# A gated linear recurrence before a mixture of experts: the next chunk's state summed by accumulating transfers, earlier due times, earlier fills

## The chip, the core and the metric

The kernel runs on one core of one Trainium2 chip. A core has TensorE (matrix products, PE in the profile), VectorE (DVE), ScalarE (ACT), GpSimd (POOL) and SyncE (SP); each executes its own instructions in order and waits on semaphores for the others. Transfers between memory and the on-chip buffers run beside them on 16 transfer engines. SyncE and GpSimd issue them here, each into a queue of its own. The metric is the time of the whole program on the device in microseconds; lower is better.

## The reference

```python
# B, H, S, D = 4, 8, 768, 48
mag = np.sqrt(a_re * a_re + a_im * a_im)
scale = np.minimum(mag, 0.999) / (mag + 1e-06)
a_re_n, a_im_n = (a_re * scale, a_im * scale)
for t in range(S):
    new_re = ar * S_re - ai * S_im          # ar, ai: a_re_n, a_im_n at t, per key dimension
    new_im = ar * S_im + ai * S_re
    S_re, S_im = (new_re + kv, new_im)      # kv: outer product of k[t] and v[t]
    y[:, :, t] = np.einsum('bhd,bhde->bhe', q[:, :, t], S_re)
...
# x: y with the heads side by side, [3072, 384]; E = 8 experts, F = 1024, cap = 768
logits = x @ w_gate
expert_idx = np.argmax(logits, axis=1)      # one expert for a token, gate_w its probability
h = np.maximum(np.einsum('ecd,edf->ecf', disp, w1), 0.0)
y = np.einsum('ecf,efd->ecd', h, w2)
out[i] = gate_w[i] * y[expert_idx[i], pos[i]]
```

The recurrence has a complex factor for each key dimension and step. Everything is float32.

## The kernel before

**Chunks and groups.** The 768 steps are cut into 8 chunks of 96 (C), two to a group, so there are four groups (0 to 3). Inside a chunk the cumulative products of the complex factors are taken outward from the chunk's middle, so that q and k can be multiplied by them and the chunk's output becomes a masked matrix product, as in linear attention. Real and imaginary parts lie side by side: 48 real and 48 imaginary rows of a state make 96 partitions.

**Slices.** For a group, all batches, heads and both directions fill 128 partitions, and the 48 steps outward are done in six slices of 8 (`SIZES`). A slice goes through `norm` (line 278: load of the factors `a`, the clipped scale by squares, logarithm and exponential on ScalarE, sums by TensorE against the identity, products on VectorE), `scan` (line 371: eight dependent complex products, lines 394 and 399, on VectorE) and `post` (line 413: q and k times the products or their inverses, lines 442 and 477 on VectorE, then writes to a scratch tensor in memory, lines 485 to 499, issued by GpSimd). The last slice's products are also taken aside by `pend` (line 524), which makes of them the factors `pcol` that carry a state into the next chunk (lines 567 to 572).

**Units.** A unit (line 576) is one chunk of one batch: 8 units to a group, 32 in all. SyncE loads its q and k from the scratch tensor (line 593), v and the middle row; TensorE turns q and k (619), multiplies them (635), VectorE masks the product (639), and TensorE multiplies that with v (700) and q with the incoming state z (705). Chunk c's state is `s` (650 on TensorE, plus z on VectorE in 659). For the next chunk it is multiplied by a complex factor: two transfers issued by SyncE exchange the real and the imaginary half into `sx` (663), `u` is s times the real factor (671 on ScalarE, eight instructions; 668 on VectorE where the next chunk is in the last group), `sx` is multiplied by the imaginary factor (674, VectorE), and the sum of both is the next z (677, VectorE). This happens 28 times: chunks 0 to 6 of four batches. A chunk's z is read four units later. In an odd chunk it needs the `pcol` of the next group, so at the border between two groups the states are carried over only when the next group's scan is done.

**Experts.** Each finished unit is routed; GpSimd sends its token rows to the buffer `disp` in memory by an indirect transfer (1007). That buffer is first filled with empty rows in seven transfers of 772 KB (`fill`, line 846), issued by GpSimd. Then the eight experts run (from line 1176 on), their weights split into two parts by ScalarE and VectorE (1112, 1113), and are bound to TensorE's work (1203, 1211, 1224).

**What sets the order.** A planner (class `Plan`) lists every operation of the attention part with an engine, an assumed duration, its predecessors, the buffers that it shares and a due time, `want`; it simulates the engines and writes the resulting order into the program. Among operations that could start at about the same time the one due earlier goes first. An operation that issues a transfer (one with `kb`) is also not placed before its due time; the others may go earlier. Due times hang on `BEGIN`: the scan of group g is due from BEGIN[g] to BEGIN[g+1], the units of group g from BEGIN[g+1] + 8 on, and the last entry sets the experts' first weight loads (BEGIN[4] + 26) and the routing's last steps. `fill_gaps` puts in matrix products of no use (line 226) where the plan shows TensorE idle, to keep it running. On the chip the engines execute this order whatever the plan's times were.

Of the kernel before, what the change touches and what calls it, by code (L numbers as in the profile page):

```python
# [18 lines left out]
C = 96  # L19
# [161 lines left out]
class Att:  # L181
# [96 lines left out]
    def norm(self, g, j, s0):  # L278
# [6 lines left out]
        w = s0 - 14  # L285
# [11 lines left out]
        def xa():  # L297
            a4 = self.tile_a4(g, j)
            sq = st['sq'] = a4[:, 0:n, 0:2, :].rearrange("p i z d -> p z i d")
            nc.scalar.activation(sq, st['a'], AF.Square, accum_out=self.sums[g][:, 0, j:j + 1])  # L300
        o = plan.op(K + ("xa",), "ACT", act(2 * n * D) + .1, xa, w, after=[K + ("load",)], bufs=[a_, a4_])
        if g == 0 and j < 1:
# [4 lines left out]
            o = plan.op(None, "DVE", dve(n * D), xb, w, after=[o], bufs=[a4_])  # L307
            parts = [(0, n, o, a4_)]
# [215 lines left out]
    def pend(self, g, want):  # L524
# [36 lines left out]
        def cols():  # L561
            pr = self.p_t.tile([C, 2, B, H], F32, tag="vgp", name=f"vgp_{g}", bufs=1)
            for i in range(int(g == 0), G2):
# [8 lines left out]
                nc.vector.tensor_tensor(out=p[1], in0=p[1], in1=pr[:, 1], op=ALU.subtract)  # L572
# [3 lines left out]
    def unit(self, g, i, w, per, near):  # L576
# [84 lines left out]
        def swap(i):  # L661
            a, o = ((slice(0, D), slice(D, None)), (slice(D, None), slice(0, D)))[i]
            nc.sync.dma_start(out=st['sx'][a], in_=st['s'][o])

        def turn():
            u = st['u'] = self.p_c.tile([C, H, D], F32, tag="u", name=f"u_{b}_{c}", bufs=2)
            if nx // G2 == NG - 1:
                nc.vector.tensor_tensor(out=u, in0=st['s'], in1=pc(0).unsqueeze(2).broadcast_to([C, H, D]), op=ALU.mult)
                return
            for h in range(H):  # L670
                nc.scalar.mul(out=u[:, h, :], in_=st['s'][:, h, :], mul=pc(0)[:, h:h + 1])  # L671

        def state_a():
            nc.vector.tensor_tensor(out=st['sx'], in0=st['sx'], in1=pc(1).unsqueeze(2).broadcast_to([C, H, D]), op=ALU.mult)

        def state_b():
            nc.vector.tensor_tensor(out=zn[:C], in0=st['u'], in1=st['sx'], op=ALU.add)
# [3 lines left out]
        if not last:  # L681
# [3 lines left out]
            x = [plan.op(None, "SP", .55, lambda i=i: swap(i), w - 20, after=[d], bufs=[R("s_sb"), R("sx")], kb=72, extra=5.) for i in range(2)]  # L685
# [3 lines left out]
            u = plan.op(None, "DVE" if late else "ACT", dve(384) if late else 1.8, turn, wz, after=[d, pcn], bufs=[R("s_sb"), R("u")])  # L689
            za = plan.op(None, "DVE", dve(384), state_a, wz, after=x + [pcn], bufs=[R("sx")])  # L690
            plan.op(K("ZB"), "DVE", dve(384), state_b, wz + 2, after=[u, za], bufs=[R("sx"), R("u"), ("z", b, c + 1)])
# [59 lines left out]
RINGS = dict(qkc=3, v=3, qT=2, kT=2, a_sb=2, z=5, s_sb=4, sx=4, u=2, xt=2, tr=2, pa=2, s=1, ad=2, y=1,  # L751
# [847 lines left out]
```

## Time and profile before

| | us |
|---|---|
| time, median of 3 runs (635.39 to 637.35) | 635.4 |
| the profiled execution, its own time | 635.5 |
| its span, from first to last instruction | 633.7 |

| engine | busy us | share of the span | instructions |
|---|---|---|---|
| TensorE | 560.3 | 88% | 4740 |
| VectorE | 473.1 | 75% | 1356 |
| ScalarE | 384.8 | 61% | 1034 |
| GpSimd | 161.7 | 26% | 237 |

The shares are averages over stages with different limits, so the stage in which something lies has to be looked at by itself. In the chain of waits a piece is a time on an engine or in a transfer that the next piece waited for. A transfer's time to landing runs from its issue to its last byte. The mean granted clock of TensorE is 0.962 of full speed.

### The profile page before, as it was taken

The page shows a single profiled execution, that of the slowest core. Times are in us where ns is not written, and L with a number is a line of the kernel's source. Part 1 is how long each engine was busy: PE and PEld are TensorE (multiplying, and loading weights), DVE is VectorE, ACT ScalarE, POOL GpSimd, SP SyncE. Part 2 cuts the span into 40 slices and gives each one's busy share as a digit, 9 for nine tenths or more (in the row PEclk, how much of TensorE's full clock was granted, in tenths as well). Part 3 has the DMA queues.
Part 4 walks back from the last instruction along what each step waited for, and adds up shares of the span by engine and source line. Part 5 has one row for each costly group of instructions (what it writes and reads, how often), then busy time and mean ns, then how long its engine had stood idle before and what let it go on. Part 6 is the DMA issues. An engine that isn't in the chain of part 4 may idle for free.

```text
span 633.7 us, 13410 instructions
## 1 busy us (share of the span) xinstructions
PE 560.3 (88%) x4740; PEld 489.7 (77%) x4740; DVE 473.1 (75%) x1356; ACT 384.8 (61%) x1034; POOL 161.7 (26%) x237
## 2 busy tenths in 40 slices
PE   2355389899999999999989999999999999999992
PEld 1122267687787877878879987999999999999992
DVE  3999978899999999999976564455755565556541
ACT  6566658888989789987555642353434444444530
POOL 2554331231235732244210521002020111202012
PEclk9776689999999999999999999999999999999997
DMA  4378699978767977778669931634545554544301
GB/s 140 88 205 262 178 266 287 218 203 221 182 185 225 265 207 198 186 200 197 150 157 223 289 103 29 207 106 134 150 141 173 160 160 150 154 152 138 100 37 38
DMA packets 75627, 108.80 MB, mean 172 GB/s; under 512 B 11715, under 2 KB 65852, under 8 KB 75552
## 3 DMA queue, kind: packets, MB, share of 16 engines
q1 hardware_dynamic: 61776, 61.50, 35.7%
q0 software_dynamic: 13776, 46.37, 25.7%
q8 instruction: 39, 0.64, 0.4%
q14 instruction: 36, 0.29, 0.2%
HBM read 71.51 MB, written 32.47 MB: 164 GB/s over the span
## 4 chain that ended last, share of the span: by engine, by line
PE 48%; DVE 27%; DMA 10%; ACT 9%; issue 3%; SPq 1%; POOL 1%; POOLq 0%; DVEq 0%; ACTq 0%
PE ph L1203 17%; PE my L1211 15%; DVE xy L394 5%; DVE a L399 3%; DMA qkc<-scr 3%; DVE qko L442 2%; DVE qko L477 2%; PE my L1224 2%; ACT u L671 2%; DMA sx<-s 2%; PE pa L635 2%; DMA scr<-qko 2%; DVE a_sb L639 2%; PE tr L619 2%; PE yt L1157 1%
## 5 line engine op out<-in xcount | busy, mean ns | idle before, releaser
L1249 ACT ACTIVATE hh<-ph 128x448 fp32r<-128x448 f32 (+7 forms) x64 | 32.6, 510 | 92.2 <-PE ph L1203 92.2
L1250 DVE SCALAR_TENSOR_TENSOR hl<-ph,hh 128x448 fp32r<-128x448 f32 (+7 forms) x64 | 37.2, 581 | 60.3 <-ACT hh L1249 59.6
L1113 DVE TENSOR_TENSOR lo<-raw,hi 128x384 fp32r<-128x384 f32 (+2 forms) x128 | 65.5, 553 | 7.0 <-ACT hi L1112 7.0
L1203 PE MATMUL ph<-xh,hi 128*128 128x448 f32 (+7 forms) x192 | 69.7, 363 | 0.0
L1168 POOL DMA_INDIRECT out_dram<-o,xr x26 | 25.7, 987 | 162.0 <-DVE o L1167 158.6
L1203 PE MATMUL ph<-xh,lo 128*128 128x448 f32 (+7 forms) x192 | 66.6, 347 | 0.0
L272 PE MATMUL n<-a,ident 128*128 128x384 f32 x92 | 41.8, 587 | 25.3 <-ACT a L300 19.2
L394 DVE TENSOR_TENSOR xy<-a 128x192 f32<-128x192 f32 (+1 forms) x193 | 60.4, 324 | 1.7 <-ACT a L364 1.1
L1112 ACT CAST hi<-raw 128x384 fp32r<-128x384 f32 (+2 forms) x128 | 59.0, 512 | 4.0 <-DMA raw<-in_moe_w_dram 4.0
L1211 PE MATMUL my<-hh,lo 128*128 128x448 f32 (+6 forms) x168 | 58.7, 350 | 0.0
L1211 PE MATMUL my<-hh,hi 128*128 128x448 f32 (+6 forms) x168 | 58.7, 349 | 0.0
L1211 PE MATMUL my<-hl,hi 128*128 128x448 f32 (+6 forms) x168 | 58.7, 349 | 0.0
L635 PE MATMUL pa<-qT,kT 128*96 128x96 f32 x512 | 54.5, 251 | 1.1 <-DVE a_sb L639 1.0
L619 PE MATMUL tr<-ident,qkc 81*96 81x81 f32 x512 | 52.1, 237 | 3.8 <-ACT ends L517 1.0
L1007 POOL DMA_INDIRECT disp<-x,idx x32 | 39.3, 1228 | 63.0 <-DVE idx L1003 28.3
L635 PEld LDWEIGHTS pa<-qT,kT 128*96 128x96 f32 x512 | 48.8, 165 | 3.1 <-DVE a_sb L639 1.3
L619 PEld LDWEIGHTS tr<-ident,qkc 81*96 81x96 f32 x512 | 41.2, 127 | 12.1 <-ACT kT L623 2.4
L399 DVE TENSOR_TENSOR a<-xy 128x96 f32<-128x96 f32 (+1 forms) x213 | 48.7, 238 | 0.7
L272 PEld LDWEIGHTS n<-a,ident 128*128 128x128 f32 x92 | 19.1, 226 | 38.4 <-ACT a L300 21.0
L272 PE MATMUL p<-qko,ident 128*128 128x384 f32 x80 | 34.1, 553 | 15.9 <-ACT qko L431 15.8
L1203 PE MATMUL ph<-xl,hi 128*128 128x448 f32 (+7 forms) x192 | 45.8, 347 | 0.0
L650 PE MATMUL s_all<-v,qkc 128*96 128x96 f32 x448 | 42.0, 247 | 2.4 <-DMA qkc<-scr 1.7
(224 smaller groups left out, 1421.5 us busy)
## 6 DMA issues: line engine op xcount, KB each, us to landing
raw<-in_moe_w_dram SPq DMA_DIRECT2D x64, 384.0 KB
qkc<-scr SPq DMA_DIRECT2D x32, 480.0 KB
scr<-qko POOLq DMA_DIRECT2D x44, 192.0 KB, 5.3
scr<-qko POOLq DMA_DIRECT2D x20, 384.0 KB, 4.6
a<-in_av_dram POOLq DMA_DIRECT2D x18, 384.0 KB, 7.5
qkin<-in_xv_dram POOLq DMA_DIRECT2D x18, 384.0 KB, 7.1
disp<-fill POOLq DMA_DIRECT2D x7, 772.0 KB, 15.5
v<-in_vp_dram SPq DMA_DIRECT2D x32, 144.0 KB
```

Source lines behind the costliest of these rows:

```text
L272: nc.tensor.matmul(out=pt[:, :m], lhsT=self.ident, rhs=t[:, h:h + m], start=i == 0, stop=i == 1)
L394: nc.vector.tensor_tensor(out=st['xy'][:, :, cs].rearrange("p (u z) d -> p u z d", u=2), in0=a4[:, s, :, cs].rearrange("p (u z) d -> p u z ...
L399: nc.vector.tensor_tensor(out=self.a4[g, j][:, s, 0:2, cs], in0=xy[:, 0:4:2, cs], in1=xy[:, 1:4:2, cs], op=ALU.add)
L619: nc.tensor.transpose(out=pt[:, h * C:h * C + NE], in_=qk[:NE, 4 * hh + h, z_ * C:z_ * C + C], identity=self.ident[:NE, :NE])
L635: nc.tensor.matmul(out=pa[:, h * C:h * C + C], lhsT=kT[:, 4 * hh + h], rhs=qT[:, 4 * hh + h], start=True, stop=True)
L650: nc.tensor.matmul(out=pss[:, h * D:h * D + m], lhsT=qk[:, h, C:2 * C], rhs=v[:, h * D:h * D + m], start=True, stop=True)
L1007: ins = nc.gpsimd.indirect_dma_start(out=self.disp, out_offset=bass.IndirectOffsetOnAxis(ap=idx[:, c:c + 1], axis=0), in_=self.row(b, c0 + ...
L1112: return (lambda: nc.scalar.copy(out=hi[i][:, s], in_=raw[i][:, s]), lambda: nc.vector.tensor_tensor(out=lo[i][:, s], in0=raw[i][:, s], in ...
L1113: lambda: nc.vector.tensor_tensor(out=lo[i][:, s], in0=raw[i][:, s], in1=hi[i][:, s].bitcast(F32), op=ALU.subtract))
L1203: nc.tensor.matmul(out=ph[:, :W], lhsT=a[:, k, fs], rhs=r[:, k, :W], start=i == 0, stop=i == len(parts) - 1)
L1211: nc.tensor.matmul(out=py[m][:, :W], lhsT=a[:, f % self.PF, ms], rhs=r[:, :W], start=f == 0 and i == 0, stop=f == NF - 1 and i == 2)
L1250: nc.vector.scalar_tensor_tensor(out=hl[:, :W], in0=ph[:, :W], scalar=0.0, in1=hh[:, :W].bitcast(F32), op0=ALU.max, op1=ALU.subtract)
```

## The change

The sum of the two parts of the next chunk's state leaves VectorE. `turn` now writes the scaled state straight into the next chunk's buffer `zn` (there is no `u` any more), `state_a` multiplies the state itself, not its exchanged copy, and two transfers issued by GpSimd add the exchanged halves of that product into `zn`. The factor's sign moves accordingly in `pend`. The due times BEGIN move forward for groups 1 to 4. A second place for accumulating transfers, in `norm`, is chosen by `g >= NACC`. The seven fills are due from 9 us on in steps of 3, were from 45 in steps of 9; the clears of the buffers' unused partitions, all in one place before, are interleaved with the first operations.

```diff
@@ norm
-        w = s0 - 14
+        by_dma = g >= NACC
+        w = s0 - (14 + 6 * by_dma)
...
+        elif by_dma:
+            def acc():
+                nc.gpsimd.dma_start(out=st['flat'][:, 0], in_=st['flat'][:, 1], accum_op=ALU.add)
+            o = plan.op(K + ("acc",), "POOL", .6, acc, w - 2, after=[o], bufs=[a4_], kb=24 * n, extra=3.)
@@ pend
-                nc.vector.tensor_tensor(out=p[1], in0=p[1], in1=pr[:, 1], op=ALU.subtract)
+                nc.vector.tensor_tensor(out=p[1], in0=pr[:, 1], in1=p[1], op=ALU.subtract)
@@ unit
         def swap(i):
             a, o = ((slice(0, D), slice(D, None)), (slice(D, None), slice(0, D)))[i]
-            nc.sync.dma_start(out=st['sx'][a], in_=st['s'][o])
+            nc.gpsimd.dma_start(out=zn[a.start:a.stop or C], in_=st['sx'][o], accum_op=ALU.add)
         def turn():
-            u = st['u'] = self.p_c.tile([C, H, D], F32, tag="u", name=f"u_{b}_{c}", bufs=2)
             if nx // G2 == NG - 1:
-                nc.vector.tensor_tensor(out=u, in0=st['s'], in1=pc(0).unsqueeze(2).broadcast_to([C, H, D]), op=ALU.mult)
+                nc.vector.tensor_tensor(out=zn[:C], in0=st['s'], in1=pc(0).unsqueeze(2).broadcast_to([C, H, D]), op=ALU.mult)
                 return
             for h in range(H):
-                nc.scalar.mul(out=u[:, h, :], in_=st['s'][:, h, :], mul=pc(0)[:, h:h + 1])
+                nc.scalar.mul(out=zn[:C, h, :], in_=st['s'][:, h, :], mul=pc(0)[:, h:h + 1])
         def state_a():
-            nc.vector.tensor_tensor(out=st['sx'], in0=st['sx'], in1=pc(1).unsqueeze(2).broadcast_to([C, H, D]), op=ALU.mult)
-
-        def state_b():
-            nc.vector.tensor_tensor(out=zn[:C], in0=st['u'], in1=st['sx'], op=ALU.add)
+            nc.vector.tensor_tensor(out=st['sx'], in0=st['s'], in1=pc(1).unsqueeze(2).broadcast_to([C, H, D]), op=ALU.mult)
...
-            x = [plan.op(None, "SP", .55, lambda i=i: swap(i), w - 20, after=[d], bufs=[R("s_sb"), R("sx")], kb=72, extra=5.) for i in range(2)]
...
-            u = plan.op(None, "DVE" if late else "ACT", dve(384) if late else 1.8, turn, wz, after=[d, pcn], bufs=[R("s_sb"), R("u")])
-            za = plan.op(None, "DVE", dve(384), state_a, wz, after=x + [pcn], bufs=[R("sx")])
-            plan.op(K("ZB"), "DVE", dve(384), state_b, wz + 2, after=[u, za], bufs=[R("sx"), R("u"), ("z", b, c + 1)])
+            za = plan.op(None, "DVE", dve(384), state_a, wz, after=[d, pcn], bufs=[R("s_sb"), R("sx")])
+            u = plan.op(None, "DVE" if late else "ACT", dve(384) if late else 1.8, turn, wz, after=[d, pcn], bufs=[R("s_sb"), ("z", b, c + 1)])
+            o = plan.op(None, "POOL", .6, lambda: swap(0), wz - 4, after=[u, za], bufs=[R("sx"), ("z", b, c + 1)], kb=72, extra=2.)
+            plan.op(K("ZB"), "POOL", .6, lambda: swap(1), wz - 4, after=[u, za], bufs=[R("sx"), ("z", b, c + 1)], kb=72, extra=2.)
@@ constants
-BEGIN = (13, 69, 143, 219, 295)
+NACC = 4
+BEGIN = (13, 67, 135, 203, 271)
@@ kernel
-            plan.op(("fill", r), "POOL", .9, lambda r=r: box['fill'][r](), 45 + 9 * r, kb=772)
+            plan.op(("fill", r), "POOL", .9, lambda r=r: box['fill'][r](), 9 + 3 * r, kb=772)
...
+                    box['fill'] = route.clear_ops()
+                    clears = att.clear_ops()
                     for i, o in enumerate(order[:cut]):
                         o.fn()
+                        if i % 2 and clears:
+                            clears.pop(0)()
                         if i == 60:
                             att.tokens()
                             route.constants(att.tokcol)
                             route.rank_constants()
-                            for op in att.clear_ops():
-                                op()
-                            box['fill'] = route.clear_ops()
```

## Rows read from the trace of the kernel before

**Rows 1.** Stretch, length, busy us of PE, PEld, DVE, ACT, POOL; clock, transfer share, GB/s.

```profile
13.00:67.00 54.00, 23.73 (x41) 11.01 (x41) 52.99 (x180) 33.45 (x72) 26.72 (x49) 0.74 0.68 194
67.00:143.00 76.00, 63.18 (x602) 50.75 (x602) 67.83 (x193) 58.54 (x166) 21.66 (x32) 0.91 0.87 228
143.00:295.00 152.00, 145.96 (x1653) 121.14 (x1653) 147.68 (x449) 138.04 (x426) 54.32 (x66) 1.00 0.76 205
295.00:319.80 24.80, 23.73 (x298) 20.48 (x296) 24.10 (x81) 14.41 (x38) 8.31 (x9) 1.00 0.71 174
330.00:370.00 40.00, 39.90 (x566) 36.66 (x565) 26.12 (x91) 22.61 (x67) 9.97 (x10) 1.00 0.78 213
410.00:634.00 224.00, 212.38 (x1219) 207.50 (x1217) 123.31 (x257) 92.31 (x205) 29.43 (x30) 0.98 0.43 130
```

**Rows 2.** Chain of waits, 318 to 329 us; columns: start, length, what.

```profile
318.84 0.97 DVE qko L477
...
320.09 6.64 DMA scr<-qko
...
326.78 1.82 DMA qkc<-scr
```

**Rows 3.** Waits of VectorE, 60 to 143 us; columns: total, times, longest.

```profile
DVE sx L674 <- DMA sx<-s: 4.2, 2, 2.5
DVE xy L394 <- ACT a L364: 2.9, 1, 2.9
```

**Rows 4.** Line 677 alone, by stretch: VectorE busy (x instructions), clock, transfer share, GB/s.

```profile
67.00:319.80 252.80, 10.96 (x20) 0.97 0.79 209
319.80:370.00 50.20, 4.42 (x8) 1.00 0.78 207
```

**Rows 5.** Timeline of VectorE, 290 to 291 us; columns: start, length, line, tile, shape.

```profile
290.47 0.54 DVE L677 TENSOR_TENSOR z<-u,sx 96x384 f32<-96x384 f32 x1
290.94 0.24 DVE L399 TENSOR_TENSOR a<-xy 128x96 f32<-128x96 f32 x1
```

**Rows 6.** Busy us by stretch, two stretches of 8 us, columns as in rows 1.

```profile
8.00:16.00 8.00, 4.67 (x8) 2.31 (x8) 5.55 (x16) 7.20 (x19) 0.00 (x0) 0.95 0.29 90
103.00:111.00 8.00, 6.89 (x74) 5.34 (x72) 5.45 (x14) 5.83 (x16) 0.00 (x0) 1.00 1.06 248
```

**Rows 7.** SyncE's longest wait for a state; GpSimd's scratch writes (busy us, mean ns).

```profile
SPq L663 <- DVE a L399: 55.8, 13, 8.4
...
L488 POOL DMA_DIRECT2D scr<-qko x40 | 28.9, 723 | 57.1 <-DVE xy L394 30.0 <-DVE a L399 17.5 <-DVE a L350 4.2
```

**Rows 8.** One group's stretch, all engines, then line 226 alone (PE, PEld).

```profile
153.00:236.00 83.00, 79.72 (x916) 65.90 (x918) 80.72 (x241) 75.00 (x230) 34.55 (x39) 1.00 0.78 209
...
153.00:236.00 83.00, 5.63 (x38) 4.79 (x38) 1.00 0.78 209
```

**Rows 9.** Transfers by issue: count, KB each, median us to landing.

```profile
scr<-qko POOLq DMA_DIRECT2D x44, 192.0 KB, 5.3
...
disp<-fill POOLq DMA_DIRECT2D x7, 772.0 KB, 15.5
...
out_dram<-o,tail POOLq DMA_INDIRECT x4, 2.4
```

**Rows 10.** Timeline of VectorE at the last hand-over between groups.

```profile
320.77 0.55 DVE L677 TENSOR_TENSOR z<-u,sx 96x384 f32<-96x384 f32 x1
...
330.31 0.55 DVE L659 TENSOR_TENSOR s<-s_all,z 96x384 f32<-96x384 f32 x1 [2.70 <-PE s_all L650]
```

**Rows 11.** Timeline of GpSimd: the last of the seven fills.

```profile
91.73 0.77 POOL L846 DMA_DIRECT2D disp<-fill  x1
```

**Rows 12.** Timeline of all engines, 12 to 28 us: the fourth slice's load, square and first product.

```profile
12.17 0.54 SPq L292 DMA_DIRECT2D a<-in_av_dram  x1
...
17.60 0.84 ACT L300 ACTIVATE a<-a 128x768 f32<-128x768 f32 x1
...
27.20 0.55 DVE L334 TENSOR_TENSOR lnn<-n,lnn 128x384 f32<-128x384 f32 x1
```

More of the change, by code (lines that the diff above doesn't have):

```diff
@@ L299, in xa @@
             sq = st['sq'] = a4[:, 0:n, 0:2, :].rearrange("p i z d -> p z i d")
+            if by_dma:
+                flat = st['flat'] = a4.rearrange("p i z d -> p (i z d)")[:, :2 * n * D].rearrange("p (z x) -> p z x", z=2)
+                sq = flat.rearrange("p z (i d) -> p z i d", d=D)
+                st[0] = sq[:, 0]
             nc.scalar.activation(sq, st['a'], AF.Square, accum_out=self.sums[g][:, 0, j:j + 1])
@@ L307, in norm @@
             o = plan.op(None, "DVE", dve(n * D), xb, w, after=[o], bufs=[a4_])
+            parts = [(0, n, o, a4_)]
+        elif by_dma:
+            def acc():
+                nc.gpsimd.dma_start(out=st['flat'][:, 0], in_=st['flat'][:, 1], accum_op=ALU.add)
+            o = plan.op(K + ("acc",), "POOL", .6, acc, w - 2, after=[o], bufs=[a4_], kb=24 * n, extra=3.)
             parts = [(0, n, o, a4_)]
@@ L748, in routing @@
             rt.scattered = o_
-RINGS = dict(qkc=3, v=3, qT=2, kT=2, a_sb=2, z=5, s_sb=4, sx=4, u=2, xt=2, tr=2, pa=2, s=1, ad=2, y=1,
+RINGS = dict(qkc=3, v=3, qT=2, kT=2, a_sb=2, z=5, s_sb=4, sx=4, xt=2, tr=2, pa=2, s=1, ad=2, y=1,
              a=3, qk=3, a4=4, ln=4, c0=2, t5=2, xy=4, qko=4, pend=1)
```

## The prediction

> **What bounds the kernel now.** The page's totals mislead here: VectorE is busy 75% of the span and TensorE 88%, but these are averages over stages. I read a table by stage first [rows 1]. From 13 to 319.8 us VectorE leads: 52.99 us busy of 54, then 67.83 of 76, 147.68 of 152 and 24.10 of 24.80. That is the attention part, where the scan, the norms and eight units' masks and states share that engine. From 330 to 370 us TensorE is busy 39.90 of 40, and from 410 on 212.38 of 224: the last eight units and the experts, neither of which the change touches. The chain of waits shows the hinge [rows 2]: the last scan group's final product on VectorE ends at 319.81, its write lands 6.64 us after 320.09, the load that reads it back takes 1.82 us, and only then does the last group's TensorE work run without a break. So whatever ends VectorE's work at 319.8 earlier moves all behind it by as much, and nothing after that point gains by less VectorE work. VectorE's waits in the one loose stage [rows 3] are two for the half-swapped state, 4.2 us, and one of 2.9 us for ScalarE.
>
> The sum is made against the profiled execution: 633.7 us of span and 1.8 around it, 635.5, which is the median of 635.4 within 0.1.
>
> **Norm sums by transfer.** This never runs: it is chosen for groups from NACC = 4 on, and the groups are 0 to 3. Cost and gain nothing; the norms' due times do not move by its 6 either.
>
> **The state's sum leaves VectorE.** There are 28 states (four batches, chunks 0 to 6), each with one 96x384 sum at line 677. 20 of them run before 319.8 us and 8 after [rows 4], so 20 count. A sum records 0.54 us, but its successor starts 0.47 us after it (290.47 to 290.94) [rows 5], and that is what it takes from the engine: 20 x 0.47 = 9.4 us. The other eight lie in a stretch where VectorE has 26.12 of 40 us in use [rows 1] and give nothing. The product that stays (line 674) reads the state itself instead of its swapped copy, so it no longer waits for a transfer. The two waits of 4.2 us go [rows 3]. VectorE executes in order, so this is real time there; late next is whatever fills the stretch: transfers at a share of 1.06 and a VectorE that has work for only 5.45 of 8 us [rows 6]. I take 3 us of the 4.2, bounds 0 and 4.2. The sign swap in the column factors is the same instruction with its operands exchanged: no time. The scaled state is written into the next chunk's buffer directly, on ScalarE (VectorE for the last group): same shape, same count.
>
> **56 transfers change queue.** SyncE loses 56 issues and the waits for the state in which later loads stood behind them (55.8 us in 13 waits of one kind alone); GpSimd gains 56 of about 0.72 us, the mean of its 40 scratch writes [rows 7]: 40 us in all, 16 x 0.72 = 11.5 in the stretch from 153 to 236 us, where it is busy 34.55 of 83 [rows 8]. Each pair waits in GpSimd's queue for the product on VectorE and the eight scalings on ScalarE; behind it stand the scratch writes, the next a and qkin loads and the token sends. The plan issues those loads some 14 us before use, and all but a group's last writes wait for nothing soon. I charge 0; without that cover it is the scalings' 1.8 us for the pair that stands before a group's last write.
>
> No accumulating transfer is in this trace. Its landing I bound by GpSimd's own transfers [rows 9]: 2.4 us for the fastest, 15.5 for the fills; nearest in size and queue is the 192 KB scratch write, 5.3 us, which I take. Before, swap came first and sum last; now the transfer comes last, so it lies between a state and its reader. At the last hand-over between groups the sum runs at 320.77 and the first reader, line 659, starts at 330.31 [rows 10]: 9.5 us of room. Two issues and a landing are 1.4 + 5.3 = 6.7 us. Inside, so 0; at the upper end 1.4 + 15.5 = 16.9 us, 7.4 us late. The Trainium skill, DMA: Bandwidth & Descriptors, section Anatomy of one DMA — SWDGE (gpsimd) path, prices a transfer from this queue at about 2.0 us plus its bytes at 436 GB/s; an estimate from that is 2.2 us for 72 KB, and the sum by it would be the same. A rule against the change is in the Trainium skill, Collectives: The Full Stack, section The bandwidth ceiling: an add in the transfer engines reads two sources and ran at half the rate of a copy there; no run here shows it yet.
>
> **Fills moved forward.** Seven fills of 772 KB, 5.4 MB, are issued up to 91.73 us now [rows 11], the last of them in the stretch where transfers are saturated, and go where their share is 0.29 [rows 6]. What they could free is the first units' loads and with them part of the 2.9 us wait [rows 3]: I take 1, bounds 0 and 2.9. What they could hurt: the fourth a load issues at 12.17 and its square starts at 17.60 [rows 12], so it landed within 5.4 us. If it landed as late as a fill, 15.5 us, ScalarE's queue would stop 10 us there, and the scan's copies stand behind it. But the stage has spare transfer time, and the first product from that slice runs on VectorE at 27.20 [rows 12], 9.6 us later; with some 4 us for the steps between, a stop of 10 would cost VectorE 4. I take 0, bounds 0 and 4. The buffer clears spread over the start run on a GpSimd that is idle there (0.00 of 8 us).
>
> **Groups begun sooner.** Due times order the work; only transfers are held until due. The last product ends 24.8 us after its group's due end of 295 [rows 2], so compute is not waiting for its date: 0, give or take 1. But the first experts' weight loads are due 26 us after the last BEGIN, and that falls from 321 to 297, while VectorE's end can fall by some 10 only. Their first two loads, 768 KB or 3.6 us at the 213 GB/s of [rows 1], may now stand on SyncE's queue ahead of the 1.82 us load of [rows 2]. I charge 1, bounds 0 and 3.6.
>
> **Coupling.** From 153 to 236 us, with 3.8 us of sums off 83, VectorE would need 79. In that stretch TensorE has 79.72 - 5.63 (matmuls that only keep it warm) = 74.1 and ScalarE 75.0 [rows 8]: 94 and 95% of 79. In-order engines that full wait for each other more than VectorE's present 2.3 us idle there. I charge 3 us over the three groups, bounds 0 and the whole 9.4.
>
> **Sum.** 635.5 - 9.4 - 3 - 1 + 1 + 3 = 626.1, forecast 626.
>
> **Rivals.**
> - *ScalarE and TensorE take over.* If coupling returns 8 of the 9.4: 635.5 - 1.4 - 3 - 1 + 1 = 631. For: 94 and 95% above. Against: much of ScalarE's busy time is set by VectorE's pace, and its queue also waits for VectorE.
> - *More than forecast.* No coupling loss, both waits of rows 3 gone, weights harmless: 635.5 - 9.4 - 7.1 = 619. For: the whole attention part is one VectorE queue. Against: the transfer share of 1.06.
> - *It cancels.* Coupling takes the 9.4 and the weights 3.6, against 3 and 1: 635.5 - 4 + 3.6 = 635.
> - *Slower: the accumulating pair lands late.* From a landing of 9.5 - 1.4 = 8.1 us on, the next group's first readers wait for the state. At the fills' 15.5 us it is 7.4 us each time: in full at the last hand-over, where VectorE idles already [rows 10], about half at the two earlier ones, where it has scan work: 14.8 in all, 626.1 + 14.8 = 641. For: the queue carries a and qkin pairs of 768 KB ahead of it. Against: 72 KB, and 5.3 us for writes through the same queue. By the rule of the Collectives page the reading side doubles; at half rate 72 KB are still few.
> - *It does not do what it says.* True of the norm part, counted above at nothing.
>
> **Numbers.** Forecast (621 to 630) 0.50; more 0.16 (616 to 621); engines take over 0.14 (630 to 633.5); cancels 0.08 (633.5 to 637.4); slower 0.12. Less than 0.3%, 1.9 us, this kernel's measurement can't tell from none. Faster 0.80, same 0.08, slower 0.12. The range 616 to 637 leaves out the slower case and the far end of the better one.
>
> **What would show it.** VectorE: no line 677, 28 fewer instructions, no wait for a swap; its last product near 310. GpSimd: 56 more transfers of 0.7 us, landing in 4 to 7. Line 659 at the last hand-over released by TensorE, not by a transfer. Transfer share over 0.5 at 8 to 32 us, and under 1 at 87 to 111. Expert stage unchanged at 224 us. Wrong if line 659 or the y matmuls wait for the accumulating transfer, if ScalarE stalls near 17 us, or if weight loads stand before the last group's first load.

## The result, and the profile after

The changed kernel takes 630.07 us (median of 7, 627.74 to 633.17) where the kernel before takes 635.61 (median of 7, 635.39 to 637.35): a ratio of 0.990 with a 95% interval of 0.988 to 0.992. The forecast was 626 in a range of 616 to 637. The profiled execution took 628.2 us, 626.5 of span and 1.7 around it, against 633.7 of span before; so the two traces differ by 7.2 us and the medians by 5.5.

**The stages.** Columns as in [rows 1]; these are the same stretches, then the two of [rows 6].

```profile
13.00:67.00 54.00, 26.52 (x42) 12.33 (x41) 51.82 (x188) 32.77 (x71) 22.59 (x58) 0.65 0.82 239
67.00:143.00 76.00, 63.85 (x632) 50.72 (x634) 72.45 (x207) 63.91 (x184) 27.08 (x39) 0.89 0.77 199
143.00:295.00 152.00, 144.93 (x1671) 120.70 (x1667) 147.89 (x465) 137.88 (x428) 89.62 (x100) 1.00 0.84 213
295.00:319.80 24.80, 22.62 (x295) 19.97 (x294) 18.51 (x49) 14.85 (x42) 10.69 (x14) 1.00 0.81 195
330.00:370.00 40.00, 39.70 (x548) 36.27 (x547) 20.94 (x114) 17.76 (x56) 13.88 (x16) 1.00 0.63 159
...
8.00:16.00 8.00, 5.09 (x8) 2.37 (x8) 5.66 (x16) 7.21 (x19) 7.94 (x16) 1.00 0.72 236
103.00:111.00 8.00, 7.84 (x89) 6.86 (x87) 8.00 (x21) 7.47 (x24) 3.90 (x6) 1.00 0.98 256
```

VectorE still leads up to the last scan product. It is fuller between 67 and 143 us (72.45 against 67.83) and as full between 143 and 295 (147.89 against 147.68): there it does 16 instructions more in the same time, since the sums are gone. Over the whole program it has 16 instructions fewer and not the 28 forecast: the 28 sums are gone, but the scan now runs in 12 more pieces (lines 404 and 409). In the stretch from 295 us on its scan work ends, at 305.37 us.

**The hinge.** The chain of waits between 302 and 321 us, which answers to [rows 2], then the first reader of the state, which answers to [rows 10].

```profile
304.40 0.97 DVE qko L487
...
305.65 7.93 DMA scr<-qko
...
313.64 2.39 DMA qkc<-scr
...
316.07 1.56 PE s_all L660 x16
```
```profile
317.67 0.55 DVE L669 TENSOR_TENSOR s<-s_all,z 96x384 f32<-96x384 f32 x1 [2.10 <-PE s_all L660]
```

The last product ends at 305.37 instead of 319.81, 14.4 us sooner. The write and the load behind it take 10.3 us instead of 8.5. The reader is released by TensorE, as forecast, and not by the accumulating transfer.

**Where the scan gained.** Each scan group ends with a copy of its state by ScalarE. These copies start at 67.98, 150.94, 233.91 and 312.87 us before, and at 70.73, 144.57, 223.68 and 298.14 after. So group 0 lost 2.75 us, group 1 gained 9.1, group 2 gained 3.9 and group 3 gained 4.5. VectorE's waits from 13 to 60 us (one row), and then from 60 to 143 us, which answers to [rows 3], say why the first two differ. Columns: total, times, longest.

```profile
DVE mask L242 <- ACT tokcol L241: 1.7, 1, 1.7
```
```profile
DVE lnn L344 <- ACT lnn L335: 2.4, 1, 2.4
DVE a_sb L649 <- PE pa L645: 0.4, 1, 0.4
```

Both waits of [rows 3], 7.1 us, are gone, and a smaller one has come. Group 0 now waits 1.7 us for the token constants, which GpSimd began to make at 2 us before and begins at 17.95 us now, behind clears and fills. That is not all of the 2.75 us: with the earlier due times alone (told of below) group 0 ends at 69.4 us, 1.4 later than before, with a wait of only 0.2 us for these constants.

**What was given back.** The 14.4 us shrink to a span that is 7.2 shorter. Behind the last product the write and load cost 1.9 us more, and the last send takes 4.29 us to land instead of 2.56 (chain of waits, before and then after):

```profile
373.38 2.56 DMA disp<-x,idx
```
```profile
361.81 4.29 DMA disp<-x,idx
```

So the first expert product comes 10.4 us sooner, not 14.4. TensorE does not idle longer for it: between the last scan product and the first expert product it is idle for 4.0 us in place of 3.6, and busy for 71.1 in place of 67.5. The scan ran ahead of it, so more of the units' matmuls are left behind the last product. How much of the 4.0 us is the transfers' and how much this work was not separated. Then the end of the program: the last store of the output is issued by GpSimd, and the span ends some time after it. Timeline of GpSimd, before and then after:

```profile
623.35 1.28 POOL L1168 DMA_INDIRECT out_dram<-o,xr  x1 [0.62 <-DVE o L1167]
```
```profile
612.91 1.27 POOL L1175 DMA_INDIRECT out_dram<-o,xr  x1 [0.62 <-DVE o L1174]
```

633.7 - 623.35 is 10.4 us; 626.5 - 612.91 is 13.6. That is 3.2 us that the forecast had no term for. Most of it, 2.4 us, is one instruction of GpSimd, a DRAIN near the program's end, which takes 5.2 us in place of 2.8; the instruction before it takes 1.46 in place of 0.88. No transfer of GpSimd's queue is under way by then: the last of the 56 is issued at 338.1 us, and the queue's last packet ends at 618.1, 2.3 us before the DRAIN starts. What it does in that time the trace doesn't show.

**The accumulating transfers.** Line 673 in the page, then its landing times, and the two big queues (packets, MB, share of 16 engines' span):

```profile
L673 POOL DMA_DIRECT2D z<-sx x56 | 47.5, 1008 | 40.4 <-PE pa L645 12.1
```
```profile
DMA to landing us min/median/max: 3.0/5.5/9.0
```
```profile
q1 hardware_dynamic: 58192, 57.37, 33.7%
q0 software_dynamic: 17360, 50.50, 29.9%
```

They land in 5.5 us (median), where 5.3 was taken. GpSimd spends 1008 ns on one (mean), not 723, and is busy 212.6 us in all instead of 161.7.

### The profile page after: what moved, and what is told of

It is laid out like the page before. It is cut to its first block, busy times and chain, and to the rows that moved or that the text cites. A ratio compares the mean times of both kernels' runs of the same rounds, so it can differ in the third digit from the quotient of the medians.

```text
span 626.5 us, 13278 instructions
## 1 busy us (share of the span) xinstructions
PE 552.8 (88%) x4662; PEld 482.1 (77%) x4662; DVE 459.2 (73%) x1340; ACT 382.8 (61%) x1034; POOL 212.6 (34%) x293
## 4 chain that ended last, share of the span: by engine, by line
PE 51%; DVE 20%; ACT 13%; DMA 8%; issue 3%; POOL 2%; SPq 0%; POOLq 0%; DVEq 0%; ACTq 0%
PE ph L1210 17%; PE my L1218 15%; DVE xy L404 4%; ACT z L680 3%; DVE a L409 3%; DMA scr<-qko 3%; PE n L272 2%; PE my L1231 2%; DMA a<-in_av_dram 2%; DVE qko L452 2%; PE pa L645 2%; ACT ends L527 2%; PE tr L629 2%; PE s_all L660 2%; DVE qko L487 1%
## 5 line engine op out<-in xcount | busy, mean ns | idle before, releaser
L272 PE MATMUL n<-a,ident 128*128 128x384 f32 x92 | 45.9, 636 | 27.7 <-ACT a L305 22.2
L673 POOL DMA_DIRECT2D z<-sx x56 | 47.5, 1008 | 40.4 <-PE pa L645 12.1
L272 PEld LDWEIGHTS n<-a,ident 128*128 128x128 f32 x92 | 20.5, 243 | 42.6 <-ACT a L305 24.0
L1014 POOL DMA_INDIRECT disp<-x,idx x32 | 42.0, 1313 | 30.8 <-DVE se L996 8.7
L272 PE MATMUL p<-qko,ident 128*128 128x384 f32 x80 | 36.6, 587 | 14.0 <-ACT qko L441 14.0
```

The lines of the kernel that those rows point to most:

```text
L272: nc.tensor.matmul(out=pt[:, :m], lhsT=self.ident, rhs=t[:, h:h + m], start=i == 0, stop=i == 1)
L673: nc.gpsimd.dma_start(out=zn[a.start:a.stop or C], in_=st['sx'][o], accum_op=ALU.add)
L1014: ins = nc.gpsimd.indirect_dma_start(out=self.disp, out_offset=bass.IndirectOffsetOnAxis(ap=idx[:, c:c + 1], axis=0), in_=self.row(b, c0 + ...
```

## The experiments

All ratios are to the kernel before on the same chip, timed beside it, with 95% intervals. The kernel before took 637.0 and 635.6 us on two of the chips and 649.7 to 650.5 on two others, so times are compared only on one chip. "Sums" stands for the memory sums, "begins" for the earlier BEGIN, "fills" for early clears and fills.

**The kernel before again**, for its trace beside the next three.

> The kernel before, profiled on the chip of this call, as the base that the one-part kernels are read against. Its group ends (the last copy of a state by ScalarE) were at 67.98, 150.94, 233.91 and 312.87 us on the first chip, the first expert product at 391.01, 78.1 us behind the last group end, and 635.4 us in all. If the 650 us that the kernel before took in the last call belongs to that chip, and it is this one again: about 650 us, with the loss in the stretch behind the last group end (89 to 95 us in the one-part kernels) and the group ends within 3 us of the first chip's. If the loss came from the edits: 78 us there and about 636 us.

It took 634.8 us. Group ends 68.0, 150.8, 233.8 and 312.8, first expert product at 390.3, 77.4 us behind the last: the first chip's numbers.

**The changed kernel again.**

> The changed kernel, on the chip of this call, beside the kernel before. If the gain is the first chip's: 0.988 to 0.992 of the kernel before (643 us where that takes 650), with group ends at 70.7, 144.6, 223.7 and 298.1 us. If the gain needs the fast transfers of the first chip: 0.997 or more, and the stretch behind the last group end takes some 95 us, as in the kernel with the memory sums alone.

Ratio 0.9886 (0.9843 to 0.9929), 631.1 us. Group ends 71.4, 146.7, 226.8 and 302.6. Its profiled execution was the slowest of its four (635.7; the others 628.5 to 631.2). The gain repeats on a second chip.

**Sums alone.** The kernel before with these lines of the change and no others:

```diff
-            nc.sync.dma_start(out=st['sx'][a], in_=st['s'][o])
+            nc.gpsimd.dma_start(out=zn[a.start:a.stop or C], in_=st['sx'][o], accum_op=ALU.add)
...
-            plan.op(K("ZB"), "DVE", dve(384), state_b, wz + 2, after=[u, za], bufs=[R("sx"), R("u"), ("z", b, c + 1)])
+            plan.op(K("ZB"), "POOL", .6, lambda: swap(1), wz - 4, after=[u, za], bufs=[R("sx"), ("z", b, c + 1)], kb=72, extra=2.)
```

> The kernel before with the state's change alone: the sum leaves VectorE and becomes two accumulating GpSimd transfers; due times, fills and clears stay as before. Theory A (VectorE is one queue up to its last product; 20 sums of 0.47 us and the 4.2 us of waits for the swapped half are what it got back): the last product on VectorE at 319.8 - 13.6 = 306 us, the first group's scan still done at 68 us, time 622 to 626. Rival B (the earlier due times or the earlier fills did it): the last product later than 314, time over 630. On the program's end: if the 56 more GpSimd transfers lengthen the stretch from the last token send to the end, it is 13 us here, as after the change; if not, 10 us as before.

Ratio 0.998 (0.9952 to 1.0008): no gain, and the last product ends at 319.0 us, not at 306 as theory A had it. The swap's wait is gone, but another has taken its place in the same stretch. VectorE's waits, 60 to 143 us:

```profile
DVE a_sb L639 <- PE pa L635: 5.5, 1, 5.5
DVE xy L394 <- ACT a L364: 1.6, 1, 1.6
```

So the 4.2 us for the swapped half were not the swap's price: what VectorE needs next in that stretch is late too. How much of the missing gain is the price of GpSimd's queue (see the swaps on that queue, below) was not separated.

**Early clears and fills alone.**

```diff
-            plan.op(("fill", r), "POOL", .9, lambda r=r: box['fill'][r](), 45 + 9 * r, kb=772)
+            plan.op(("fill", r), "POOL", .9, lambda r=r: box['fill'][r](), 9 + 3 * r, kb=772)
...
+                        if i % 2 and clears:
+                            clears.pop(0)()
```

> The kernel before with the fills and clears moved forward alone. Theory A: the first group's scan is done 2 to 3 us later (VectorE waits for the token constants that GpSimd now makes behind clears and fills), and the waits of VectorE between 90 and 115 us, 7.1 us before, shrink to 2 to 5; the rest keeps its length: 632 to 636. Rival B (the fills are what freed VectorE): under 630. The stretch from the last send to the end stays 10 us.

Ratio 0.9934 (0.9909 to 0.9959). VectorE has no wait for a swapped half here either, though every swap is in place; its waits between 90 and 115 us add up to 4.7 us, as expected. Group 3 ends at 313.6 us, so this gain doesn't lie in the scan, unless the scan of the kernel before, not traced on this chip, ends later here than on the two chips where it was.

**Earlier begins alone.**

```diff
-BEGIN = (13, 69, 143, 219, 295)
+BEGIN = (13, 67, 135, 203, 271)
```

> The kernel before with the earlier due times alone. Theory A: compute isn't waiting for its date, so the last product stays within 2 us of 319.8 and the time within 633 to 639, the upper end if the experts' first weight loads get ahead of the last group's first load. Rival B (groups begun sooner is where the gain is): the last product before 314, time under 630.

Ratio 1.0248 (1.0206 to 1.029): some 16 us slower, and both expectations missed. Most of the loss is in group 1, which ends at 163.1 us in place of 151. TensorE there, in order:

```profile
92.82 1.29 PE L619 MATMUL tr<-ident,qkc 81*96 81x81 f32 x8 [5.76 <-issue]
...
99.71 0.59 PE L272 MATMUL n<-a,ident 128*128 128x384 f32 x1
```

The earlier due time puts the first units' transposes (line 619, units of group 0) ahead of the scan's own matmul (line 272, for group 1) in TensorE's queue; in the kernel before that matmul runs at 90.12 us, ahead of them. The transposes wait for their load, which SyncE issued at 78.25 us and which lands at 92.7; the scan waits behind them, and VectorE runs dry. The busy table for 88 to 96 us shows it, here first, and then in the kernel with begins and fills, told of below:

```profile
88.00:96.00 8.00, 3.18 (x22) 3.20 (x23) 0.99 (x4) 2.29 (x6) 0.00 (x0) 0.50 1.02 252
```
```profile
88.00:96.00 8.00, 7.96 (x65) 6.51 (x63) 5.88 (x27) 6.32 (x17) 1.11 (x2) 0.78 0.56 147
```

With the fills still at 60 to 108 us the transfer engines are full (1.02) and VectorE works 0.99 us of 8; with the fills out of the way the share is 0.56 and it works 5.88. Full transfer engines alone don't do it: the kernel before has a share of 1.09 in this stretch and VectorE works 4.96 us, since its order puts the scan's matmul first.

**Sums and begins, late fills**: the changed kernel with the fill lines above put back.

> The changed kernel without the early clears and fills: memory sums and earlier groups. Alone the sums measured 0.998 and the earlier groups 1.025 of the kernel before. Theory A, they need each other: the sums leave VectorE 8 x 0.47 us a group, which only earlier due times turn into earlier work, and earlier due times without room on VectorE only push the scans aside; together they give 5 to 6 us, a ratio of 0.990 to 0.993, and the fills add the 2 to 4 us that they give alone. Theory B, the earlier groups need the early fills (the GpSimd queue with clears and fills in the way of the first swapped halves at the new begin times): 1.01 or more, with the loss between 67 and 143 us. Theory C, parts add up: 0.998 + 0.025, about 1.02.

Ratio 1.0145 (1.0065 to 1.0224). Theory B: the begins need the early fills. Group 1 ends at 159.7 us, and VectorE works 0.26 us of 8 between 88 and 96. Its profiled execution was the slowest of its four (655.1 us; the others 642.8 to 652.3). Theory C's 1.02 is inside the interval too, but the full change at 0.9886 refutes adding up: 0.998 x 0.9934 x 1.0248 would be 1.016.

**Sums and fills, old begins**: the changed kernel with BEGIN put back.

> The changed kernel with the old begin times: memory sums and early fills. Theory A: without earlier due times the sums buy nothing, as alone (0.998), so the ratio is that of the early fills alone, 0.991 to 0.996. Theory C, parts add up: 0.9934 x 0.998 = 0.991. Theory D, the earlier begin times cost something in every company, and the whole change would do better without them: 0.985 or less, faster than the changed kernel by over 0.3%.

Ratio 0.9969 (0.9949 to 0.999). Group 3 ends at 305.2 us, 7.6 sooner than in the kernel before on that chip, yet the span is only 0.4 shorter: the way from there to the first expert product is 4.2 us longer and the program's end 3.0 longer. Theory A is just missed, and theory D, better without the begins, is out.

**Begins and fills, no sums**: the last of the eight combinations, the kernel before with the two edits shown above.

> The kernel before with early clears and fills and the earlier begin times, without the memory sums: the missing one of the eight combinations. The forecast's reason gives the sums nearly all of the gain (20 sums of 0.47 us, 9.4 us): then this kernel is at 1.000 to 1.006 of the kernel before, and its group ends are some 4 us later each from group 2 on than the changed kernel's spacing of 79 us (83 us as before). Rival theory, the two waits of 7 us in group 1 and the order are all of the gain, and VectorE would have had the time for the sums: 0.987 to 0.992. By the three one-part runs and the pair runs so far neither is excluded: the sums took 1% where the begin times were early (1.0145 against 1.0248) and nothing where they were not.

Ratio 0.9999 (0.9972 to 1.0025). The rival, that the sums were not needed, is out. The profiled execution, 655.2 us, was the slowest of ten. VectorE's waits, 60 to 143 us:

```profile
DVE lnn L334 <- ACT lnn L325: 2.3, 1, 2.3
DVE a_sb L639 <- PE pa L635: 2.0, 1, 2.0
```

Here the swaps by SyncE are all in place, and no wait for one is left. And the scan's pace, from the first to the last copy of a state (the times behind the comma), in this kernel and then in the changed one on the first chip:

```profile
L534 ACT COPY pend<-a x4: 251/254/258, 71.3 to 311.0; 128x96 f32<-128x96 f32 x4
```
```profile
L544 ACT COPY pend<-a x4: 254/256/268, 70.7 to 298.1; 128x96 f32<-128x96 f32 x4
```

239.7 us against 227.4; the repeat of the changed kernel has 231.2. So the sums are worth 8.5 to 12.3 us of scan, with 9.4 forecast; against the changed kernel with later weights (below), on the same chip as this one, it is 239.7 against 228.5, 11.2 us. Between the ends of groups 1 and 3 alone it is 163.0 against 153.6, 9.4 us, and 155.9 in the repeat, 7.1. VectorE is busy 157.1 us of it here (157.3 in the kernel before) and 149.5 and 149.9 in the changed one.

Together:

```
sums begins fills   ratio   95% interval       group 3 ends at (us)
 -     -     -      1                           312.8
 x     -     -      0.998   0.9952 to 1.0008    311.9
 -     -     x      0.9934  0.9909 to 0.9959    313.6
 -     x     -      1.0248  1.0206 to 1.029     324.5
 x     -     x      0.9969  0.9949 to 0.999     305.2
 x     x     -      1.0145  1.0065 to 1.0224    316.2
 -     x     x      0.9999  0.9972 to 1.0025    311.0
 x     x     x      0.9886  0.9843 to 0.9929    302.6
```

The last column, read in pairs, says where the sums pay in the scan. They bring group 3's end forward by 8.4 us with early fills, under the old due times (313.6 to 305.2) and the new ones (311.0 to 302.6) alike, by 8.3 with early due times and late fills, and by 0.9 alone. The rows come from three chips, and the changed kernel itself ended group 3 at 298.1 on the first chip and 302.6 in the repeat, so differences of a few us are not to be read.

**The swaps on GpSimd's queue, nothing summed.**

```diff
-            nc.sync.dma_start(out=st['sx'][a], in_=st['s'][o])
+            nc.gpsimd.dma_start(out=st['sx'][a], in_=st['s'][o])
...
-            x = [plan.op(None, "SP", .55, lambda i=i: swap(i), w - 20, ...
+            x = [plan.op(None, "POOL", .6, lambda i=i: swap(i), w - 20, ...
```

> The kernel before with the 56 swaps issued by GpSimd in place of SyncE, as plain copies; all 28 sums stay on VectorE. Theory A: no VectorE work goes, so 632 to 637; what leaves SyncE's queue gives at most the 4.2 us of swap waits. Rival C (SyncE's blocked queue was what held the units back): under 630. For the program's end: a stretch of 13 us from the last send if the number of GpSimd transfers lengthens it, 10 us if only accumulating ones do or neither.

Ratio 1.0085 (1.0047 to 1.0124), slower than either expectation. It prices the queue: 56 more issues on GpSimd without the sums' gain cost 0.9%. Group 3 ends at 316.4 us, 3.5 later than on the first chip, and the program's end takes 2.1 us more. A plain transfer of 72 KB holds GpSimd for about half as long as an accumulating one:

```profile
L663 POOL DMA_DIRECT2D sx<-s x56: 502/520/557, 96.1 to 344.2; - x56
```
From the last store's issue to the end of the span, all traces together:

```
no transfers added to GpSimd's queue       10.4, 10.4, 10.4, 10.7, 10.4 us   (before, its repeat, fills, begins, begins + fills)
56 plain ones                              12.5 us
56 accumulating ones                       13.6, 13.0, 13.7, 13.2, 13.4, 13.3, 13.6, 13.4 us
```

That splits by the number and kind of GpSimd's transfers and by nothing else that was varied. The 56 plain ones add 896 packets of 4608 bytes to the queue, the 56 accumulating ones 2688 of 1536, so number of packets and kind can't be told apart here.

**Clears behind the constants.** The changed kernel with

```diff
-                        if i % 2 and clears:
+                        if i > 60 and i % 2 and clears:
```

> The changed kernel with the fills early and the clears of the rings' spare rows behind the 60th planned operation, so that GpSimd makes the token constants before them. Theory: group 0's end at 70.7 to 71.4 us (68.0 before) comes from VectorE's wait of 1.7 us for these constants; here that wait is gone, group 0 ends at 68 to 69.5 us, and the run takes 1.5 to 2.5 us less than the changed kernel (ratio 0.984 to 0.986 where that measured 0.9886); group 1's first loads still land on time, since it is the fills and not the clears that share the DMA engines with them. Rival, the clears are what must be out of the way: group 1 ends later than 149 us and the ratio is 0.995 or more. Rival, room at the start is taken back at the next hand-over: group 0 earlier, group 3 within 1 us of the changed kernel's, ratio as the changed kernel's.

Ratio 1.0032 (0.9999 to 1.0066): the theory missed. The first rival's numbers came true (group 1 ends at 152.6 us), but not for its reason: group 1 itself takes 74.9 us, as in the changed kernel (73.8, and 75.3 in the repeat), and the loss is in group 0. Without clears between them five fills are issued from 2.94 to 6.89 us, and a load of the scan stands among them. Chain of waits:

```profile
11.94 12.45 DMA a<-in_av_dram
```

Group 0 ends at 77.7 us, 7 later than in the changed kernel, and the token constants come no sooner (at 28.5 us, in the changed kernel 21.6), since TensorE's step in their making stands behind that load. So the clears have a use nobody wrote down: they space the fills.

**Weights later.** The changed kernel with

```diff
-    t0 = BEGIN[NG] + 26
+    t0 = BEGIN[NG] + 50
```

> The changed kernel with the experts' first weight loads due 24 us later (BEGIN[NG] + 50 in place of + 26), so that they don't stand before and beside the last hand-over's loads. The forecast put the cost of these loads at 1 us (bounds 0 to 3.6). Theory: the write and the load of the last hand-over took 7.93 and 2.39 us in the changed kernel and 6.64 and 1.82 before, 1.9 us more, because the weight loads share the DMA engines with them: here they take 8.5 us together, and the end comes 1 to 2 us sooner (ratio 0.985 to 0.988). Rival: the weights are then late at the experts' start (waits of ScalarE for raw weights at 370 to 385 us) and the ratio is 0.990 to 0.995. Rival: the longer write is the accumulating transfers' doing, then it stays 7.5 us or more.

Ratio 0.9846 (0.9806 to 0.9886). At the last hand-over the state's summing matmul starts 8.9 us after the last write's issue ends (316.72 against 307.84), where it is 316.07 against 306.4, 9.7, in the changed kernel and 328.74 against 320.84, 7.9, in the kernel before. ScalarE waits for no weights at the experts' start, so that rival is out. This is the fastest version: faster than the kernel before for sure, but its interval overlaps that of the changed kernel (0.9843 to 0.9929), so that it beats that one isn't shown.

**Fills between, weights later.** The last with clears as in the kernel before and

```diff
-            plan.op(("fill", r), "POOL", .9, lambda r=r: box['fill'][r](), 9 + 3 * r, kb=772)
+            plan.op(("fill", r), "POOL", .9, lambda r=r: box['fill'][r](), 24 + 4 * r, kb=772)
```

> The changed kernel with three things put elsewhere: the clears behind the token constants in one piece, as in the kernel before; the seven fills due at 24 + 4r us, so behind the loads of the first slices (the last of which lands at 18 us) and still ahead of group 1's first loads at 80 us; the experts' first weight loads due 24 us later. Theory: all that the fills need is to be out of the DMA engines' way at both places. Then group 0 ends at 68 to 69 us (68.0 in the kernel before, 70.7 to 71.4 in the changed one), group 1 at 142 to 144 us, no wait on VectorE between 67 and 143 us is over 3 us, and the ratio to the kernel before is 0.979 to 0.984, where the late weights alone measured 0.9846 and the changed kernel 0.9886. Rival, the changed kernel's fills between 7 and 26 us are needed that early: group 0 late by 2 us or more or group 1's loads late again, ratio 0.985 to 1.00. Rival, the time won at group 0 is taken up at the last hand-over: group 0 ends by 69 us and the ratio is 0.985 to 0.989.

Ratio 0.9978 (0.9957 to 1.0). The first rival. The fills are issued from 35 to 54 us, four of them in the first 5 us, and the next slice's load pays:

```profile
40.91 14.42 DMA a<-in_av_dram
```

Group 0 ends at 72.9 us, and group 3 at 303.6, so the scan keeps most of its gain. The rest is lost behind it: 98.7 us to the first expert product.

## Why the prediction was right, point by point

**The bound.** Right up to the last product, which VectorE's scan sets. That all behind it moves by as much is not right: the last product comes 14.4 us sooner and the first expert product 10.4 (380.57 against 391.01), since the write, the load and the last send take longer and TensorE has more left to do in between. Only the experts themselves are rigid: from their first product to the last store's issue it takes 232.4 to 232.6 us in all fourteen traces.

**The norm part** never ran, as said: no such transfer is in the trace.

**The state's sum, 9.4 us.** Right in size: 7.1 to 9.4 us between the ends of groups 1 and 3, where 16 of the 20 sums lie (7.5 us). VectorE is busy 7.4 to 7.8 us less there. But the forecast let this gain stand by itself, and it doesn't: alone the sums move group 3's end by 0.9 us and the time not at all. With the early fills and the old due times they do move group 3's end, by 8.4 us, and it is lost behind it.

**The waits, 3 us of 4.2.** The size was too small and the cause wrong. I gave this to the sums, because the product no longer reads a swapped copy. The kernels with the fills alone and with begins and fills keep every swap and have no such wait, and the one with the sums alone has a wait of 5.5 us in its place. The fills took the wait away. Both waits of [rows 3] went, 7.1 us, where the forecast had 3 for one and 1 for the other.

**The queue change, 0.** Right at the hand-over: 5.5 us to land against 5.3 taken, and the reader waits 2.1 us for TensorE and not for the transfer. Outside GpSimd's own queue one wait for such a transfer is left in the trace, 1.0 us of TensorE's line 711, which is what the forecast named as a sign against it; it is small. The rival of a late pair is out. The issues were not free, though: priced by the swaps alone they put group 3's end 3.5 us later (on another chip), and an accumulating one takes 1008 ns where 0.72 us was taken. Of the packets, a plain one of 1536 bytes took 65 ns in this trace (median), an accumulating one 139. The Trainium skill, Collectives: The Full Stack, section The bandwidth ceiling, says an add reads two sources and ran at half a copy's rate; by that rule, the trace agrees, at 139 / 65 = 2.1. Its DMA: Bandwidth & Descriptors, section Anatomy of one DMA — SWDGE (gpsimd) path, gave the estimate of 2.2 us for 72 KB; here the trace differs, 3.0 at the fastest and 5.5 at the median.

**What the queue change costs at the end** was no step of the forecast: 3.2 us. I charged the issues against GpSimd's neighbours in time and never asked what they leave behind for the program's end. It is the one term that was missing altogether; why the end grows with them stays open.

**The fills, 1 us.** Mis-sized. Alone they give 0.7%, and with the begins they are the difference between 1.0145 and 0.9886. The step looked at the wait that they cause in the kernel before, and not at what a reordered TensorE would have to wait for beside them. Their cost at the start, bounds 0 to 4 us, was charged at 0: group 0 lost 2.75, of it 1.7 in a wait for the token constants behind the fills and none by the slice's load, which I had watched; with the begins alone group 0 loses 1.4, so the rest may be theirs. The load is a danger all the same: 12.45 us when nothing spaces the fills.

**The begins, 0 give or take 1.** Wrong by themselves: +2.5%. The forecast said that due times order the work, and then priced them only as dates. They are places in TensorE's order, and as each engine executes in order, the scan paid for a load that wasn't there: 5.76 us of TensorE in the rows above. In the company of the early fills they are worth having: 0.9886 (up to 0.9929) with them, 0.9969 (from 0.9949) without.

**The weights, 1 us.** Write and load took 1.9 us longer. Moving the weights took back about 0.8 of it, so the size was near. The other half is not explained; the kernel with the sums alone, whose weights come as late as before, needs 9.2 us by the same measure, so the sums may have a part in it. The sign named against the forecast, weight loads ahead of the last group's first load, came true without the sums: two stand there in the kernels with begins alone and with begins and fills, and ScalarE waits 4.5 and 2.7 us for them.

**Coupling, 3 us.** Too much. Groups 2 and 3 gained 3.9 and 4.5 us for 8 sums of 0.47, 3.8 us, each, with TensorE and ScalarE near full beside them; in the repeat they gained 3.0 and 3.2, 1.3 us short of the sums. The rival that these two engines take over is out as far as the last product; behind it TensorE's own work may have kept some of the 4.0 us.

**The sum.** To the last product the forecast had -9.4 - 3 - 1 + 3 = -10.4 and got -14.4; behind it +1 and got +7.2 (1.9 for write and load, 1.7 for the last send, 3.2 for the program's end, 0.4 spread). It came out near because two errors of 4 and 6 us have opposite signs; that is luck. By the medians the gain is 5.5 us, little more than half of the 9.4 forecast.

**Open.** From the end of group 3 to the first expert product it takes 77 to 86 us in five of the traces (before, after, their repeats, and sums with fills) and 89 to 101 us in the nine others, all of them on the two slower chips but one. What parts them is the granted clock: in this stretch it is at its lower level, 1.2 GHz, for 0 to 3.4 us in the five and for 10 to 24 us in the nine. Busy table of this stretch for the kernel before and for the one with the fills alone, with nearly the same number of matmuls:

```profile
312.87:391.00 78.13, 74.15 (x919) 64.25 (x919) 50.03 (x192) 38.09 (x114) 18.07 (x19) 1.00 0.65 171
```
```profile
313.62:403.00 89.38, 82.81 (x925) 70.04 (x922) 49.94 (x192) 37.96 (x113) 19.17 (x20) 0.94 0.55 149
```

Why the clock falls is not settled. In six of the nine TensorE stops for 4 to 7.5 us there, VectorE and ScalarE mostly stop with it, and the clock falls during it; in the kernel with the fills alone it falls without any stop of TensorE over 0.9 us. Two stretches of the kernel with the sums alone, busy table:

```profile
355.00:360.00 5.00, 2.52 (x36) 1.96 (x32) 1.04 (x2) 0.73 (x2) 3.78 (x5) 0.93 0.77 222
360.00:365.00 5.00, 0.00 (x0) 0.00 (x0) 0.00 (x0) 0.05 (x1) 2.48 (x3) 0.50 0.40 119
```

In the kernel with sums and begins ScalarE waits 5.75 us for a weight load there, and TensorE behind it; in the other five what the engines wait for is not in the records, where the releaser is another core, an unknown queue or none. The kernel before takes 14 us more on those two chips as well, so a slower chip is not the change's doing, but its trace there was not taken, and where it loses the 14 us isn't known. Four of these nine traces are also the slowest executions of their kernels. The 0.7% of the fills alone, and what the last experiment lost, seem by the group ends to lie in this stretch and are left unexplained.

## What to carry to other kernels

Work taken off the leading engine can pay nothing by itself: here it paid in the scan only once loads or due times had moved too, and in the time only where the due times had. Three edits that change the time by -0.2% (no more than its interval), -0.7% and +2.5% one by one change it by -1.1% together, so test such edits in company before any is dropped. A due time in a kernel of in-order queues is a place in an order; before moving one, ask which load its first instruction needs and what shares the transfer engines with that load. And when transfers change queue, look at the end of the program too: here it grew with what had been issued on GpSimd's queue 280 us earlier.

## What was not expected of the hardware

- The end of the program takes longer with more transfers on GpSimd's queue, though all had landed by then: 10.4 to 10.7 us from the last store's issue, 12.5 with 56 plain transfers more, 13.0 to 13.7 with 56 accumulating ones.
- An accumulating transfer of 72 KB holds GpSimd for 1008 ns at issue (mean); a plain one of the same size held it for 520 (median, swaps on GpSimd's queue).
- A load of the scan beside a burst of four or five 772 KB fills took 12.45 us (issued by SyncE) and 14.42 (issued by GpSimd behind the fills); with the fills spaced by clears ScalarE waited 0.6 us for it (the changed kernel's repeat).
- The same kernel took 635.6 and 637.0 us (medians) on two chips and about 650 on two others.
